# Out-projection of chunks 2 to 5 by a 26-product scheme on 4x4 by 4x2 blocks, with ten right forms made once, stored in DRAM and streamed

## The chip, the cores and the metric

The kernel runs on one core of a Trainium2 chip. The metric is the device time of one execution in microseconds; three executions of the kernel before took 994.28, 994.46 and 996.12 us, and the median, 994.46, is its time. The core has five instruction queues that run at the same time and wait for each other by semaphores: TensorE (PE in the profile; PEld is its weight load), VectorE (DVE), ScalarE (ACT), GpSimd (POOL) and SyncE (SP), which here only issues DMA transfers. SBUF is the on-chip memory that all of them work from; PSUM is the small memory that TensorE writes its products to, in eight banks.

## What is computed

The reference has two parts. A routed attention over 4 batches, 8 heads, 768 positions and 64 columns per head gives a matrix x of 3072 tokens by 512 columns. The second part, which the change touches, is

```python
h = x @ w_in                                   # 3072x512 @ 512x2048
sp = np.maximum(h, 0.0) + np.log1p(np.exp(-np.abs(h)))   # softplus
g = h * erf(sp)
return (g @ w_out).astype(np.float32)          # 3072x2048 @ 2048x512
```

All of it is in fp32. Softplus and erf are two ScalarE tables, and each change of table is an instruction of its own.

## The kernel before

The attention fills the span up to about 410 us. While it runs, the weights are loaded and some of their sums are made. Then comes the second part, in six chunks (`NCHUNK`) of 512 tokens.

**Products by sevens.** Both matrix products are done by a seven-product scheme for matrices cut into 2x2 blocks: seven products of sums of blocks (`ORDER` gives their sequence) take the place of eight products of blocks. `left_forms` and `right_forms` make the sums, four additions each, and put three into new places and one in place of a block. `block` (line 649) runs seven products: for each it takes a PSUM bank, issues the matmuls, evicts the bank as `fresh` or `further` say (copies by ScalarE, additions by VectorE), and then does the next one or two entries of `aside_work`, a list of side work for the other engines that is written out by hand.

**Hidden.** `hidden(n, lot)` (line 668) makes the hidden units of chunk n in one of two lots (halves of the 2048). It has four blocks of seven products, each product two matmul calls. The hidden values lie transposed, features on the partitions, in two tiles `g` per lot, one for each half s of the chunk's tokens. The right operand is x and its three new sums in `x_more`.

**Gate.** `gate` runs softplus and erf on ScalarE over one `g` tile and multiplies on VectorE. `add_hidden` then makes the left sums of the gated values, on VectorE, into a tile `g_more`.

**Project.** `project(n, lot, pace)` (line 720) multiplies by `w_out`: for each s one block of seven products of four matmul calls each, so that a chunk has 2 lots x 2 halves x 7 = 28 products. `w_out` stays in SBUF with block b12 replaced by b22 - b12, and its three new sums stay in `more_out`; these forms are made once, on GpSimd. The second lot is added to the first in `osb`, from where SP stores it.

**Order.** The main loop (line 990) alternates so that a gate always has a stage of matmuls beside it:

```python
project(n, 0, 2 if n else 3)
...
hidden(n + 1, 0)
...
project(n, 1, 2)
...
hidden(n + 1, 1)
```

The sums of the next chunk's x (`right_forms(ve, *x_parts(n + 1))`) are VectorE side work of the first project stage. Each engine runs its instructions in the order in which they are written: the class `InOrder` (line 55) records every operation, which is why nearly all instructions of the profile have line 62, and are told apart by the tiles that they write and read. DMA issues by `nc.sync` are placed by the framework.

Of the kernel before, what the change touches and what calls it, by code (L numbers as in the profile page):

```python
# [2 lines left out]

# [6 lines left out]
F32 = mybir.dt.float32  # L10
# [4 lines left out]
ALU = mybir.AluOpType  # L15
ACT = mybir.ActivationFunctionType
# [3 lines left out]
P = 128  # L20
B, H, S, D = 4, 8, 768, 64
C = 16
# [9 lines left out]
DM, DFF = H * D, 2048  # L32
NFT = DFF // P
CT = 512
NCHUNK = B * S // CT
HT, HK, HF, HM = CT // 2, DM // P // 2, NFT // 2, DM // 2
FG = HF // 2
# [11 lines left out]
LAST_X = 11  # L49
MASKS = {(0, 2): ("k", 0), (2, 0): ("q", 0), (2, 2): ("k", 1), (5, 2): ("q", 1)}  # L50
FIRST_MASKS = {(2, 0): ("k", 0), (2, 1): ("q", 0), (2, 2): ("k", 1), (5, 2): ("q", 1)}


class InOrder:
# [16 lines left out]
def kernel(  # L71
# [10 lines left out]
    nc = tc.nc  # L82

    in_order = [True]
    te, ve, ae, ge = (
        InOrder(tc, e, in_order) for e in (nc.tensor, nc.vector, nc.scalar, nc.gpsimd)
    )

    def pool(name, bufs, **kw):
        return ctx.enter_context(tc.tile_pool(name=name, bufs=bufs, **kw))  # L90
# [3 lines left out]
    dram = pool("dram", 1, space=bass.MemoryType.DRAM)  # L94
# [4 lines left out]
    w_out = const.tile([P, NFT, DM], F32, name="w_out")  # L99
    more_in = const.tile([P, 3, HK, DFF // 2], F32, name="more_in")  # L100
    more_out = const.tile([P, 3, HF, HM], F32, name="more_out")
# [95 lines left out]
    for base, pattern, sign, op, fill in (  # L197
# [5 lines left out]
            out=first, in_=first, compare_op=op, fill=fill, base=base, pattern=pattern,  # L203
# [61 lines left out]
    for e in range(2):  # L265
        for n in range(2):
            r = e * D + n * Q
# [275 lines left out]
    def load_x(n):  # L543
        if n < NCHUNK:
            if n not in x_of:
                x_of[n] = xp.tile([P, DM // P, CT], F32, name="x_own")
            nc.sync.dma_start(
                out=x_of[n], in_=x_dram.rearrange("(k p) t -> p k t", p=P)[:, :, n * CT : (n + 1) * CT]
            )
# [52 lines left out]
    g_of = {}  # L602
# [10 lines left out]
    aside_work = []  # L613
# [49 lines left out]
    def finish_aside():  # L663
        for work in aside_work:
            work()
        aside_work.clear()

    def hidden(n, lot, between={}, pace=1, **kw):

        for s in range(2):  # L670
            g_of[n, s, lot] = gp.tile([P, 2, FG, HT], F32, name="g")
        x = rights(*x_parts(n))
        for j in range(FG):
            w = lefts(*w_in_parts(lot * FG + j, 1))
            a, b = (g_of[n, s, lot] for s in range(2))
            block(
                lambda i: [(w[i][:, k], x[i][:, k]) for k in range(HK)],
                fresh(a[:, 0, j], b[:, 0, j], a[:, 1, j], b[:, 1, j], **kw), pace=pace,
            )
            between.get(j, lambda: None)()  # L680
# [22 lines left out]
    def idle(n):  # L703
        return [lambda: None] * n

    def gates(n, lot, which=(0, 1), between=()):
        work = list(between)
        for s in which:
            curves, products_of = gate(n, lot, s)
            if s == which[0]:  # L710
                work = [curves] + work + idle(7 - len(work)) + products_of
            else:
                work += [curves, *sums, *idle(3)] + products_of
            sums = add_hidden(n, lot, s)
        return work + sums

    out_v = out.rearrange("(n t p) m -> n p t m", p=P, t=2)
    osb_of = {}

    def project(n, lot, pace):  # L720

        w = rights(*w_out_parts(lot * FG, FG))
        for s in range(2):
# [17 lines left out]
            block(lambda i: [(g[i][:, f], w[i][:, f]) for f in range(FG)], after, done, pace)  # L741
            del g_of[n, s, lot], sums_of[n, s, lot]

    def run(work):
        for _ in work:
            pass
# [16 lines left out]
    def period(p, i):  # L763
# [4 lines left out]
        def mask(place):  # L768
            which = (MASKS if p else FIRST_MASKS).get((i, place))
            if which:  # L770
# [108 lines left out]
    for e in range(2):  # L879
        ve.tensor_copy(  # L880
            out=ccT[e * D : (e + 1) * D, :, e * C : (e + 1) * C],
            in_=pct[e * D : (e + 1) * D].rearrange("d (r e c) -> d r e c", e=2, c=C)[:, :, e],
# [7 lines left out]
    for r in (0, D):  # L890
        for half in range(2):
            for e in range(2):
                c = r + half * Q + e * C
                ve.tensor_copy(
                    out=pick[r : r + D, half, e * D : (e + 1) * D].rearrange("p (n c) -> p n c", n=2)[:, :, 1 : C + 1],
                    in_=first[r : r + D, c : c + C].unsqueeze(1).to_broadcast([D, 2, C]),
# [49 lines left out]
    gsp = pool("gsp", 4)  # L946
    actp = pool("actp", 1)
    outp = pool("outp", 2)
# [38 lines left out]
    aside_work += together(idle(2) + gates(0, 0, (0,)), all_weights(4, N_LATE))  # L987
    hidden(0, 1, pace=2, first=ve.tensor_copy)
    finish_aside()
    for n in range(NCHUNK):  # L990
        between = right_forms(ve, *x_parts(n + 1)) if n + 1 < NCHUNK else []
        if n == 0:
            aside_work += gates(0, 0, (1,), between) + gates(0, 1, (0,))
        else:
            aside_work += gates(n, 1, (0, 1), between)
        project(n, 0, 2 if n else 3)
        finish_aside()
        if n == 0:
            aside_work += together(gates(0, 1, (1,)), idle(2) + [fence] + out_forms[2] + out_forms[3])
            hidden(1, 0, first=ve.tensor_copy)  # L1000
        elif n + 1 < NCHUNK:
            hidden(n + 1, 0)
        if n + 1 < NCHUNK:
            finish_aside()
            load_x(n + 2)
            aside_work += gates(n + 1, 0)
        project(n, 1, 2)
        finish_aside()
        if n + 1 < NCHUNK:
            hidden(n + 1, 1)  # L1010
            finish_aside()


# [30 lines left out]
```

## Time and profile before

| What | Before |
|---|---|
| median of three runs | 994.46 us |
| profiled execution, its own time | 994.52 us |
| span of that execution, first to last instruction | 992.8 us |
| TensorE busy, from 409.5 us on | 580.3 of 583.3 us |
| VectorE, ScalarE, GpSimd busy there | 365.0, 200.3, 35.6 us |
| TensorE waits after 412 us | none in the table of waits |
| VectorE: 128x256 eviction from PSUM; 128x512 sum or product in SBUF | 0.42; 0.68 us |
| GpSimd: 128x512 sum of fp32 | 1.27 us |
| ScalarE: table load; 128x2048 softplus or erf; 128x256 copy | 1.28; 1.91; 0.37 us |
| 512 KB load from DRAM; 256 KB store, issue to landing | 3.4 to 4.7; 2.0 us |

TensorE is busy from the first product of the second part to the last, so the other engines' busy shares matter only where TensorE comes to wait for them. A row of the timeline gives start, length, engine, line, operation, the tile written, the tiles read, shapes and a count of equal instructions in a row. In the groups "128x512" counts what one instruction covers. The matmul rows overlap, since matmuls are pipelined; the distance between two starts is what one costs.

### The profile page before, as it was taken

How to read it: one execution, taken by the hardware profiler on the slowest of the kernel's cores; microseconds unless marked ns; L12 is line 12 of the kernel's file. 1: busy time of each engine (PE TensorE's matmuls, PEld its weight loads, DVE VectorE, ACT ScalarE, POOL GpSimd, SP SyncE). 2: the span in 40 equal slices, each digit the busy share in tenths (PEclk: the TensorE clock that was granted, in tenths of full speed). 3: DMA queues.
4: the chain of work that ended last, by engine and by line, in shares of the span. 5: the costliest groups of instructions: out<-in, count | busy, mean ns of one | idle time of the engine just before them, and what ended most of it. 6: DMA issues, size and time to landing. Idle time of an engine off the chain costs nothing.

```text
span 992.8 us, 20557 instructions
## 1 busy us (share of the span) xinstructions
PE 985.6 (99%) x8362; PEld 739.5 (74%) x8362; DVE 709.1 (71%) x1361; ACT 488.1 (49%) x659; POOL 350.6 (35%) x237
## 2 busy tenths in 40 slices
PE   8999999999999999999999999999999999999998
PEld 3555555555555555788888888888888888888887
DVE  8888888888888886889666564756475647655653
ACT  3777777777776665485432414150505050505050
POOL 1688888787888888662400000000000000000000
PEclk9999999999999999999999999999999999999999
DMA  9444444444444210331000100010001000000001
GB/s 217 83 111 108 109 109 111 108 115 108 92 96 110 52 35 18 101 111 61 1 22 22 43 1 22 22 43 1 22 22 43 1 21 22 1 1 22 22 1 42
DMA packets 147294, 55.88 MB, mean 56 GB/s; under 512 B 128640, under 2 KB 137088, under 8 KB 147200
## 3 DMA queue, kind: packets, MB, share of 16 engines
q1 hardware_dynamic: 144848, 54.29, 21.9%
q8 instruction: 65, 1.06, 0.5%
q10 hardware_dynamic: 2352, 0.30, 0.2%
q14 instruction: 29, 0.24, 0.1%
HBM read 41.98 MB, written 12.58 MB: 55 GB/s over the span
## 4 chain that ended last, share of the span: by engine, by line
PE 98%; DVE 1%; DMA 0%; issue 0%; ACT 0%; SPq 0%; DVEq 0%
PE bank L62 44%; PE turned L62 32%; PE sc L62 16%; PE wide L62 6%; DVE nmx L62 1%; DMA in_q<-in_q_dram 0%; DVE sims L62 0%; DVE kT L62 0%; DVE qT L62 0%; DVE km L62 0%; DVE turned L62 0%; DVE nbig L62 0%; ACT qm L62 0%; DVE osb L62 0%; SPq L62 0%
## 5 line engine op out<-in xcount | busy, mean ns | idle before, releaser
L62 POOL TENSOR_TENSOR more_out<-more_out,pr 128x768 f32<-128x768 f32 x128 | 217.2, 1697 | 18.6 <-ACT pr L62 10.1
L62 DVE TENSOR_REDUCE nmx<-wide 128x2 f32<-128x768 f32 x189 | 180.5, 955 | 48.2 <-PE wide L62 47.2
L62 ACT ACTIVATE pr<-sc 128x768 f32<-128x768 f32 x192 | 149.0, 812 | 94.3 <-PE wide L62 78.6
L62 PE MATMUL turned<-pr,in_v 128*32 128x194 f32 x3072 | 145.4, 330 | 0.0
L62 PEld LDWEIGHTS turned<-pr,in_v 128*32 128x32 f32 x3072 | 91.5, 109 | 51.2 <-issue 21.3
L62 DVE TENSOR_TENSOR g<-bank,g 128x256 f32<-128x256 f32 x222 | 89.7, 421 | 53.1 <-PE bank L62 46.3
L62 PE MATMUL bank<-x_own,w_in 128*128 128x256 f32 x424 | 104.4, 379 | 0.0
L62 PE MATMUL bank<-w_out,g 128*128 128x256 f32 x448 | 103.2, 379 | 0.0
L62 PE MATMUL sc<-qT,kT 64*128 64x384 f32 x528 | 98.3, 486 | 0.0
L62 PEld LDWEIGHTS bank<-w_out,g 128*128 128x128 f32 x448 | 85.0, 190 | 11.9 <-DVE g L62 0.4
L62 PEld LDWEIGHTS bank<-x_own,w_in 128*128 128x128 f32 x424 | 80.4, 190 | 11.5 <-issue 0.6
L62 DVE TENSOR_TENSOR osb<-bank,osb 128x256 f32<-128x256 f32 x87 | 35.5, 420 | 72.8 <-ACT osb L62 25.4
L62 ACT COPY g<-bank 128x256 f32<-128x256 f32 x28 | 10.4, 372 | 153.2 <-PE bank L62 148.5
L62 ACT ACT_TABLE_LOAD x48 | 61.6, 1283 | 45.7 <-DVE g L62 45.1
L62 PE MATMUL bank<-x_more,more_in 128*128 128x256 f32 x296 | 76.0, 379 | 0.0
L62 POOL TENSOR_TENSOR more_out<-pr,pr 128x768 f32<-128x768 f32 x32 | 60.3, 1883 | 28.3 <-ACT pr L62 28.3
L62 PEld LDWEIGHTS <-qv 64*128 64x128 bf16 x384 | 27.0, 93 | 52.9 <-issue 36.7
L62 PEld LDWEIGHTS sc<-qT,kT 64*128 64x128 f32 x528 | 50.0, 187 | 21.3 <-ACT inv L62 2.3
L62 PE MATMUL wide<-kv,qv 64*128 64x384 bf16 x378 | 64.1, 328 | 1.3 <-DVE nmx L62 0.6
L62 PE MATMUL bank<-more_out,g_more 128*128 128x256 f32 x272 | 64.3, 379 | 0.0
L62 DVE TENSOR_TENSOR g<-a_s,g 128x512 f32<-128x512 f32 x96 | 62.5, 689 | 1.2 <-ACT a_s L62 1.2
L62 PE MATMUL wide<-km,qm 64*128 64x384 bf16 (+1 forms) x378 | 62.6, 327 | 0.0
(172 smaller groups left out, 1671.7 us busy)
## 6 DMA issues: line engine op xcount, KB each, us to landing
x_own<-in_moe_w_in_dram SPq DMA_DIRECT2D x13, 512.0 KB, 4.5
in_v<-in_v_dram SPq DMA_DIRECT2D x32, 192.0 KB, 3.0
x_dram<-more_out SPq DMA_DIRECT2D x128, 48.0 KB, 2.0
x_own<-x_dram SPq DMA_DIRECT2D x6, 1024.0 KB, 5.2
out_dram<-osb SPq DMA_DIRECT2D x23, 256.0 KB, 2.0
in_k<-in_k_dram SPq DMA_DIRECT2D x59, 96.0 KB, 2.8
in_q<-in_q_dram SPq DMA_DIRECT2D x58, 96.0 KB, 2.8
g_more<-in_moe_w_out_dram SPq DMA_DIRECT2D x6, 512.0 KB, 3.4
```

The lines of the kernel that those rows point to most:

```text
L62: ins = getattr(self.engine, name)(*args, **kw)
```

## The change

Chunks 0 and 1 stay as they were, except that the two project stages of chunk 1 now follow each other. Chunks 2 to 5 run `hidden26(n, 0)`, `hidden26(n, 1)` and then `project26(n)`, one projection for both lots. The gated values of a chunk are taken as 4 token blocks by 4 feature groups (left operands 0 to 15), `w_out` as 4 feature groups by 2 column halves (`w_block` 0 to 7), and the product as 4 by 2 blocks (c 0 to 7). The list `RIGHT` gives for each of 26 products the right operand: a block of `w_out` (negative), one of eight kept forms (0 to 7: six places in `more_out` and two blocks of `w_out` overwritten), or one of ten streamed forms (100 to 109). `LEFT` gives the left operand, which may be one of three extra places (16 to 18). Twenty-eight `LEFT_STEPS` per chunk make left forms in place, each after the product named first in its entry (-3 and -1: before the first product), four on GpSimd (`POOL_STEPS`) and the others on VectorE. `AFTER` says how each product goes into the output: c copies and a adds the bank, C and A do so from another output place or one of three temporaries (8 to 10).

The forms of `w_out` are made once, in the hidden stages of chunk 2 (`forms26`): four GpSimd instructions first put b12 back, then eighteen forms in two pieces each run on GpSimd, or on VectorE for six of them. Ten go by way of a ring of three SBUF places to a DRAM tensor, and in each projection they are loaded back into the ring, three ahead.

In `hidden26` the gate works on half of the four feature blocks of both token halves at a time. The last quarter of the gate is in `project26`: its curves after product 0, its four products of VectorE after products 4 and 5. The x sums of the next chunk move from VectorE to GpSimd, into the projection.

```diff
+KAPPA = {1: (0, 1), 2: (0, 0), 0: (1, 1), 3: (1, 0)}
+FORM_STEPS = [
+    (0, -2, -8, 1, -1), (10, -4, -8, -1, 7), (9, -5, -6, -1, 3), (1, -3, -5, -1, -1), (2, -6, 1, 1, -1),
+    (9, -4, 2, -1, 0), (9, -7, 1, -1, 5), (6, -1, -5, 1, 1), (3, -6, 10, -1, -1), (4, 10, 6, -1, -1),
+    (9, 1, 0, -1, 4), (7, -7, -8, -1, 8), (6, -6, 6, -1, -1), (9, -2, 6, 1, 2), (10, -7, 10, 1, 6),
+    (5, -7, 0, -1, -1), (9, -1, 5, 1, 9), (7, -3, 10, -1, -1),
+]
+VECTOR_FORMS = (3, 4, 6, 10, 15, 16)
+RIGHT = [
+    2, 7, -3, 100, -6, 3, 101, 4, -1, 102, 6, 103, 0,
+    104, -4, -7, 105, 1, 106, 5, 107, -1, 108, -2, -2, 109,
+]
+LEFT = [
+    17, 13, 18, 9, 2, 17, 6, 2, 17, 12, 14, 9, 5,
+    10, 1, 3, 7, 16, 14, 1, 9, 6, 1, 8, 12, 0,
+]
+LEFT_STEPS = [
+    (-3, 16, 2, 10, 1), (-3, 17, 9, 16, 1), (-1, 18, 1, 17, 1), (2, 17, 6, 14, -1), (3, 6, 5, 6, 1),
+    (4, 2, 14, 6, -1), (5, 17, 12, 14, -1), (6, 12, 0, 12, -1), (7, 14, 14, 12, 1), (8, 10, 10, 14, 1),
+    (8, 9, 9, 10, 1), (9, 5, 5, 7, 1), (10, 10, 11, 5, 1), (11, 9, 3, 15, -1), (11, 14, 13, 9, -1),
+    (11, 1, 1, 14, -1), (13, 7, 7, 11, 1), (14, 16, 16, 10, -1), (16, 0, 0, 8, 1), (16, 1, 11, 0, -1),
+    (17, 9, 9, 2, 1), (18, 6, 4, 6, -1), (18, 6, 0, 6, 1), (19, 13, 13, 15, 1), (19, 1, 1, 13, 1),
+    (20, 8, 8, 11, -1), (21, 4, 4, 5, -1), (21, 12, 12, 4, 1),
+]
+POOL_STEPS = (5, 6, 8, 10)
+AFTER = [
...
+    [('c', 9, -1, 1), ('C', 1, 9, 1), ('A', 8, 9, -1), ('A', 5, 8, 1), ('C', 9, 8, -1)],
...
+DONE = {0: 15, 6: 20, 7: 23, 1: 23, 5: 23, 3: 24, 4: 25, 2: 25}
+N_STREAM = 10
+RING = 3
...
+    ring, extra = [], []
+    b_dram = dram.tile([N_STREAM, P, FG * HM], F32, name="b_dram")
+
+    def w_block(b):
+        lot, h = KAPPA[b // 2]
+        f = h * HF + lot * FG
+        return w_out[:, f : f + FG, (b % 2) * HM : (b % 2 + 1) * HM]
+
+    def slot(i):
+        if i < 6:
+            return more_out[:, i // 2, (i % 2) * FG : (i % 2 + 1) * FG]
+        return w_block((4, 7)[i - 6]) if i < 8 else ring[i - 8]
+
+    def flat(t):
+        return t.rearrange("p f m -> p (f m)")
+
+    def take_places():
+        tiles = [
+            gsp.tile([P, 3, FG, P], F32, name="g_more").rearrange("p a j t -> p (a j t)") for _ in range(4)
+        ]
+        for t in tiles[:RING]:
+            ring.append(t[:, 0 : FG * HM].rearrange("p (f m) -> p f m", f=FG))
+            extra.append(t[:, FG * HM :].rearrange("p (j t) -> p j t", j=FG))
+        extra.append([tiles[RING][:, i * HM : (i + 1) * HM] for i in range(3)])
+
+    def forms26():
+        work = []
+        for f in (0, 2, 4, 6):
+            b12, b22 = w_out[:, f : f + 2, HM:], w_out[:, HF + f : HF + f + 2, HM:]
+            work.append(functools.partial(minus_of, b12, b22, b12, ge))
+        turns26 = itertools.cycle((9, 8))
+        for n, (o, a, b, sign, k) in enumerate(FORM_STEPS):
+            o = next(turns26) if o == 9 else o
+            out_, a_, b_ = (slot(x) if x >= 0 else w_block(-1 - x) for x in (o, a, b))
+            form = plus_of if sign > 0 else minus_of
+            engine = ve if n in VECTOR_FORMS else ge
+
+            def piece(f, out_=out_, a_=a_, b_=b_, form=form, engine=engine, k=k):
+                c = slice(f, f + 2)
+                form(out_[:, c], a_[:, c], b_[:, c], engine)
+                if f and k >= 0:
+                    nc.sync.dma_start(out=b_dram[k].rearrange("p (f m) -> p f m", f=FG), in_=out_)
+
+            work += [functools.partial(piece, f) for f in (0, 2)]
+        return work
+
+    def load_stream(k):
+        nc.sync.dma_start(out=flat(ring[k % RING]), in_=b_dram[k % N_STREAM])
+
+    def left26(n, i):
+        if i >= 16:
+            return extra[i - 16]
+        lot, h = KAPPA[i % 4]
+        t = i // 4
+        return g_of[n, t // 2, lot][:, h, :, (t % 2) * P : (t % 2 + 1) * P]
+
+    def left_step(n, x):
+        _, o, a, b, sign = LEFT_STEPS[x]
+        form = plus_of if sign > 0 else minus_of
+        form(left26(n, o), left26(n, a), left26(n, b), ge if x in POOL_STEPS else ve)
+
+    def gate26(n, lot, half):
+        gs = [g_of[n, s, lot][:, :, 2 * half : 2 * half + 2].rearrange("p h j t -> p h (j t)") for s in range(2)]
+        box = []
+
+        def curves():
+            t = actp.tile([P, 2 * FG * HT], F32, name="a_s")
+            box.append(t)
+            for s in range(2):
+                ae.activation(
+                    out=t[:, s * 1024 : (s + 1) * 1024].rearrange("p (h j) -> p h j", h=2),
+                    in_=gs[s], func=ACT.Softplus,
+                )
+            ae.activation(out=t, in_=t, func=ACT.Erf)
+
+        def product(s, h):
+            c = slice((2 * s + h) * 512, (2 * s + h + 1) * 512)
+            ve.tensor_tensor(out=gs[s][:, h], in0=box[0][:, c], in1=gs[s][:, h], op=ALU.mult)
+
+        return curves, [functools.partial(product, s, h) for s in range(2) for h in range(2)]
+
+    def gate_work(n, lot, half):
+        curves, products_of = gate26(n, lot, half)
+        return [curves, *idle(8), *products_of]
+
+    def hidden26(n, lot, generation=()):
+        generation = list(generation)
+
+        def paired(work):
+            if not generation:
+                return work
+            both = []
+            for w in work + idle(14 - len(work)):
+                g = generation[:1]
+                del generation[:1]
+                both.append(lambda w=w, g=g: [f() for f in (w, *g)])
+            return both
+
+        def middle():
+            finish_aside()
+            aside_work.extend(paired(gate_work(n, lot, 0)))
+
+        if lot:
+            aside_work.extend(paired(gate_work(n, 0, 1)))
+        else:
+            aside_work.extend(paired([]))
+        hidden(n, lot, {1: middle})
+        finish_aside()
+        return generation
+
+    def project26(n):
+        for s in range(2):
+            osb_of[n, s] = outp.tile([P, 2, DM], F32, name="osb")
+        temps = extra[3]
+
+        def c_at(i):
+            if i >= 8:
+                return temps[i - 8]
+            t = i // 2
+            return osb_of[n, t // 2][:, t % 2, (i % 2) * HM : (i % 2 + 1) * HM]
+
+        curves, gate_products = gate26(n, 1, 1)
+        gate_products = [gate_products[i] for i in (3, 1, 0, 2)]
+        between = right_forms(ge, *x_parts(n + 1)) if n + 1 < NCHUNK else []
+        for p, r in enumerate(RIGHT):
+            m = bank()
+            lhs = left26(n, LEFT[p])
+            g26 = N_STREAM * (n - 2) + r - 100
+            rhs = ring[g26 % RING] if r >= 100 else slot(r) if r >= 0 else w_block(-1 - r)
+            for f in range(FG):
+                te.matmul(m, lhsT=lhs[:, f], rhs=rhs[:, f], start=(f == 0), stop=(f == FG - 1))
+            if r >= 100:
+                if g26 + RING < N_STREAM * (NCHUNK - 2):
+                    load_stream(g26 + RING)
+            for x, step in enumerate(LEFT_STEPS):
+                if step[0] == p:
+                    left_step(n, x)
+            for op, d, src, sign in AFTER[p]:
+                dst = c_at(d)
+                source = m if op in "ca" else c_at(src)
+                if op in "cC":
+                    if 1 <= p < 6:
+                        if sign > 0:
+                            ve.tensor_copy(out=dst, in_=source)
+                        else:
+                            ve.tensor_scalar(out=dst, in0=source, scalar1=-1.0, scalar2=None, op0=ALU.mult)
+                    elif sign > 0:
+                        ae.copy(out=dst, in_=source)
+                    else:
+                        ae.activation(out=dst, in_=source, func=ACT.Copy, scale=-1.0)
+                else:
+                    (plus_of if sign > 0 else minus_of)(dst, dst, source)
+            if p == 0:
+                curves()
+            if p in (4, 5):
+                for f in gate_products[(p - 4) * 2 : (p - 4) * 2 + 2]:
+                    f()
+            if p in (12, 13, 14, 15) and between:
+                between.pop(0)()
...
+            if p == 12:
+                load_x(n + 2)
...
-    for n in range(NCHUNK):
+    for n in range(2):
         between = right_forms(ve, *x_parts(n + 1)) if n + 1 < NCHUNK else []
         if n == 0:
             aside_work += gates(0, 0, (1,), between) + gates(0, 1, (0,))
@@ -998,17 +1233,30 @@
         if n == 0:
             aside_work += together(gates(0, 1, (1,)), idle(2) + [fence] + out_forms[2] + out_forms[3])
             hidden(1, 0, first=ve.tensor_copy)
-        elif n + 1 < NCHUNK:
-            hidden(n + 1, 0)
-        if n + 1 < NCHUNK:
             finish_aside()
-            load_x(n + 2)
-            aside_work += gates(n + 1, 0)
+            load_x(2)
+            aside_work += gates(1, 0)
         project(n, 1, 2)
         finish_aside()
-        if n + 1 < NCHUNK:
-            hidden(n + 1, 1)
+        if n == 0:
+            hidden(1, 1)
             finish_aside()
+            load_x(3)
+    take_places()
+    generation = forms26()
+    for n in range(2, NCHUNK):
+        generation = hidden26(n, 0, generation)
+        generation = hidden26(n, 1, generation)
+        for work in generation:
+            work()
+        generation = []
+        if n == 2:
+            for k in range(RING):
+                load_stream(k)
+        for x, step in enumerate(LEFT_STEPS):
+            if step[0] < 0:
+                left_step(n, x)
+        project26(n)
 
 
 # ---- launch: one core; inputs and outputs as the reference has them ----
```

## The prediction

> **What bounds the kernel now.** I read the busy times first, then the chain that ended last, then the engines' timelines in the last three fifths of the span, where the change lies.
>
> ```profile
> PE 985.6 (99%) x8362; PEld 739.5 (74%) x8362; DVE 709.1 (71%) x1361; ACT 488.1 (49%) x659; POOL 350.6 (35%) x237
> ...
> PE 98%; DVE 1%; DMA 0%; issue 0%; ACT 0%; SPq 0%; DVEq 0%
> ```
>
> TensorE sets the end: it is 98% of the chain, and the table of waits has no wait of TensorE at all after 412 us. So a product taken away is worth its whole length, and any new wait of TensorE is added in full. TensorE's timeline gives the length:
>
> ```profile
> 747.88 1.89 PE L62 MATMUL bank<-w_out,g 128*128 128x256 f32 x8
> 749.61 1.89 PE L62 MATMUL turned<-w_out,g 128*128 128x256 f32 x8
> ```
>
> A product of the out-projection is 8 matmul records and starts 1.73 us after the one before. VectorE's timeline at the end of a hidden stage shows how late the last eviction is (the next TensorE stage began at 699.54):
>
> ```profile
> 699.74 0.42 DVE L62 TENSOR_TENSOR g<-g,bank 128x256 f32<-128x256 f32 x1 [0.44 <-PE bank L62]
> ```
>
> (That is 0.20 us after TensorE has gone on; here nobody waits for it.) The third reading is VectorE beside GpSimd, two timelines of the same stretch:
>
> ```profile
> 396.45 2.12 DVE L62 TENSOR_TENSOR more_in<-w_in 128x512 f32<-128x512 f32 x1
> 398.60 2.06 DVE L62 TENSOR_TENSOR more_in<-more_in,w_in 128x512 f32<-128x512 f32 x1
> ...
> 449.75 1.72 DVE L62 TENSOR_TENSOR g_more<-g 128x512 f32<-128x512 f32 x1
> ...
> 451.73 0.67 DVE L62 TENSOR_TENSOR g_more<-g_more,g 128x512 f32<-128x512 f32 x1
> ```
>
> ```profile
> 396.34 3.78 POOL L62 TENSOR_TENSOR more_out<-more_out,pr 128x768 f32<-128x768 f32 x2 [0.32 <-ACT pr L62]
> ...
> 449.63 1.30 POOL L62 TENSOR_TENSOR w_out<-w_out,osb 128x512 int32<-128x512 int32 x1 [4.49 <-DVE w_out L62]
> ```
>
> The same 128x512 operation on VectorE takes 0.67 us alone and 1.72 to 2.12 beside GpSimd. At 449.75 it ends 0.55 after GpSimd's (449.63 + 1.30 = 450.93, against 451.47). GpSimd pays too: its two 768-wide instructions take 3.78 where two alone take 3.39 (mean 1697 ns in the groups). In the old kernel this costs nothing, because after 494 us GpSimd does no work.
>
> **What the Trainium skill says.** "SBUF — State Buffer", section "Who interferes with whom": a VectorE instruction with two SBUF inputs contends with a GpSimd instruction that reads SBUF; one with at most one SBUF input doesn't. The rows above agree (2.12 against 0.67), and evictions from PSUM stay at 0.42 beside GpSimd. "TensorE: Matmul & The Clock Gate", section "What's actually happening": after an idle window of some 3.4 us the array runs at half its clock until a busy window has passed. No trace of before shows it, as TensorE never rests there.
>
> **The change, part by part.** I laid the built program's order out engine by engine and gave each instruction the duration of its nearest row; the places below are from that table.
>
> *Removed.* A chunk's out-projection has 26 products for 28: 2 x 1.727 = 3.45 us, in four chunks **-13.8 us**. Hidden products are the same 56 per chunk.
>
> *The first product's left operand (four times).* Before, a hidden stage and the next project stage overlap, since another lot was always ready. Now the first product reads form 17, the second of two sums that stand on VectorE behind the last eviction, and behind the last gate product of the lot. Counting from where TensorE would have gone on: the eviction starts at 0.20 in the row above, but a 512-wide gate product, placed between evictions, pushes it to about 0.83; form 16 starts 0.34 later (1.17), form 17, which needs it, 0.72 later (1.89) and ends at 2.57; a weight load of 0.19 and the handover make 2.8. Nothing covers it, for TensorE's queue is in order: 4 x 2.8 = **+11.2 us**. Bounds: 2.0 each if the gate product is out of the way, 3.3 if one more eviction is in it.
>
> *GpSimd inside the projection (chunks 2 to 4).* Four left steps and, new there, the four right forms of the next chunk's x run on GpSimd at 1.27 us each. The x forms wait for no product, so they follow the last left step at once, though they are written at products 12 to 15. VectorE has in this stretch, products 9 to 13, about five instructions with two SBUF inputs that each meet one of GpSimd's. A pair then takes 1.27 - 0.13 + 0.55 = 1.7 instead of 0.34 to 0.60, so 5 x 1.1 = 5.6 us late. What is late next: three dependent left steps (form 9, 14, 1), of which the third is the left operand of product 14, wanted there with some 0.9 us to spare. Evictions have eight banks (8 x 1.73 = 13.8 us) of cover; a left step has none. About 0.5 us of it is already lost in two small waits at products 11 and 12. So 3.6 at product 14 and 0.5 before it: 3 x 3.6 + 4 x 0.5 = **+12.8 us**. The old trace has no such stretch, so the bounds are wide: 0 if the five miss each other, some 19 if GpSimd's pairs run at 2.1 as they did with 768 columns. Chunk 5 has no x forms, and only the 0.5.
>
> *The ten stored forms, once, in chunk 2.* 28 GpSimd instructions and 12 of VectorE go along hidden(2,0) and hidden(2,1), 48.4 us of TensorE. GpSimd alone needs 28 x 1.27 = 36 us. But after eight of them it stands still for some 8 us until VectorE makes the form that its ninth needs, which in VectorE's order lies behind 15 or so evictions (13 us after the stage began). The other 20, half of them at 1.23 from start to start and half at 1.7 beside VectorE's two-input work, take about 28, so they end 41 us into the stage. VectorE's next-to-last form writes a ring slot whose earlier content must have been stored. That store stands on SP behind a load that waits for another store: GpSimd's form, 15 or 16 of the 20, ends at 34.6, store 3.2, load issue, store 3.2 gives 41.4 (the trace shows 3.4 for 512 KB loads and 2.0 for 256 KB stores; a 512 KB store I put at 3.2, between 2.6 and 4). VectorE reaches that form at about 37 and is held 4.6 us; behind it in its queue stand the evictions of this hidden stage. Eight banks of 0.86 us cover 6.9, and VectorE had lost some of that to GpSimd already, so TensorE loses about 4.5 us inside the stage. Then the gate of the lot's first half starts late, its ScalarE chain (two table loads of 1.28, two softplus of 1.03 by the 0.86 ns per element of the rows, erf of 1.91: 6.5 us) holds the copy that the last seven products' evictions start from, and VectorE has seven evictions, four gate products and two sums after it, some 6 us. TensorE waits about 7.7 at the chunk's first product, of which 2.8 is counted: 4.5 + 4.9 = **+9.4 us**. Bounds: 3 if the stores take 2.6 and the port costs half, 14 if they take 4.
>
> *That wait and the clock.* 7.7 us of idle hold a whole window, so by the skill the next 3.4 us or more run at half clock. Bounds: 0 and 3.4; I take **+2 us** (an estimate from that page).
>
> *Edits at nothing.* Streamed right forms: each load is issued at least 6 products ahead (10 us against 3.4). Stores of the output: VectorE work finished, SP free. The last gate in products 0 to 5: table loads, softplus and erf end at about 9 us, VectorE reaches the gate products at product 4 (8.6), GpSimd's step for product 8 ends near 13.5 of 13.8. If that cover goes, product 8 waits some tenths, which are in the 0.5 above. VectorE's load in a projection, 40 instructions at 0.34 to 0.46 and 26 at 0.60 to 0.72, is 33 of 45 us. Leaving out hidden(2,0) between the two projections of chunk 1 costs nothing: its gates are done three products before they are read. At the end two dependent sums instead of one before the last store: **+0.8 us**.
>
> *Sum.* -13.8 + 11.2 + 12.8 + 9.4 + 2 + 0.8 = **+22.4 us**. The profiled execution took 994.52 us, 1.7 more than its span of 992.8, and stands 0.06 from the median, 994.46. 994.5 + 22.4 = 1016.9; I forecast **1016 us**.
>
> **The rivals.**
>
> *A, the port doesn't bite.* If GpSimd's instructions fall where VectorE works from PSUM, the 12.8 goes to nothing and the hold inside chunk 2's hidden stage to about 0.5; the late gate still costs 4.9. Then -13.8 + 11.2 + 5.4 + 0.8 = +3.6, with the clock perhaps +2: 998 to 1001. For it: many VectorE instructions read PSUM. Against it: 26 of a projection's VectorE instructions are 512 wide with two SBUF inputs, and the doubled rows above.
>
> *B, the left steps are in time (faster).* One mechanism: VectorE runs so far ahead at each projection that its left steps come before TensorE asks for them, so only the bare chain at the opening is left, 2 us a chunk: -13.8 + 8 + 0.8, that is 989.5 us. It decides once all waits of TensorE in the four chunks together stay under 13.8 us. Against it: the opening alone, which no early work can shorten because VectorE's order is fixed, takes 8 to 11 of the 13.8.
>
> *C, the clock falls at more gaps.* If waits of 2.8 to 3.6 also let the clock drop, up to seven more losses of 1.7: 1022 to 1029. Against it: these waits hardly fill one window of 3.4.
>
> *D, the change saves no products.* The order of the built program has 104 matmul instructions per projection for 112, so this one is out.
>
> **How the numbers follow.** The port's cost as worked out, 0.64: 1007 to 1022 (stalls of chunk 2 and of product 14 from half to one and a quarter of the value, clock 0 to 3.4). A 0.19: 997 to 1004. B 0.08: 987 to 994. C 0.09. The range that leaves out 2 in 10 runs from 999 to 1024, as A's lower part and B lie below it and C's upper part above. A difference under 0.2%, 2 us, can't be told from none with this kernel. Faster by more than that is most of B: 0.07; within it, the rest of B and the lowest edge of A: 0.05; slower 0.88.
>
> **What would show each step.** TensorE's matmul records fall by 64 (2 products x 8 x 4). The table of waits, empty for TensorE now, shows waits on VectorE's `g_more` near 2.8 us in chunks 3 to 5 and near 7 in chunk 2, and on `g` of 3 to 4 us in three projections but not in the last. VectorE's 128x512 rows with SBUF inputs have means over 0.9 where GpSimd works. If TensorE's waits sum to less than 20 us, the port was priced too high; if the opening waits are under 2 us, VectorE's order is not what I read; if TensorE waits for DMA in the projections, the stream was too slow, which I don't expect.

## The result, and where the 30 us came from

The changed kernel takes 1024.51 us, the median of four runs (1023.75 to 1026.41), against 994.44 for the kernel before: a ratio of 1.0301, 95% interval 1.0283 to 1.0319. That is 30.1 us slower, where 22 were forecast, and 0.5 us above the range, which is less than the runs differ among themselves. The profiled span went from 992.8 to 1022.9 us, also 30.1.

The page of the changed kernel, busy times first and then the chain that ended last by engine:

```profile
PE 984.6 (96%) x8298; PEld 731.3 (71%) x8298; DVE 769.6 (75%) x1421; ACT 511.8 (50%) x735; POOL 430.4 (42%) x293
...
PE 84%; DVE 9%; issue 2%; POOL 2%; ACT 1%; DMA 1%; SPq 0%; DVEq 0%; POOLq 0%; ACTq 0%
```

TensorE has 64 matmul records fewer (8298 for 8362), yet its busy time fell by 1.0 us only, not by the 13.8 that 64 matmuls at 0.216 us take. That points to matmuls that run slower, though the ends of matmuls are modelled, so that busy time alone can't say by how much. And the chain, 98% TensorE before, now passes for 9% of the span through VectorE. The table of waits of TensorE after 412 us, empty before, reads (us in total, times, longest; `bank` and `turned` are PSUM tiles that a product is written to):

```profile
PE bank L120 <- DVE g_more L120: 11.1, 3, 6.2
PE turned L120 <- DVE g L120: 8.8, 2, 5.4
PE bank L120 <- DVE g L120: 6.7, 2, 3.4
PE turned L120 <- DVE g_more L120: 2.5, 1, 2.5
PE bank L120 <- ACT g L120: 0.5, 1, 0.5
```

The `g_more` rows are the openings of the four projections. The `g` rows are product 14 of chunks 2 to 4, three waits of 3.4, and one of 5.4 inside chunk 2's hidden stage. TensorE's timeline at product 14 of chunk 2 and at the opening of chunk 3:

```profile
695.98 3.30 PE L120 MATMUL turned<-w_out,g 128*128 128x256 f32 x8 [3.37 <-DVE g L120]
699.08 2.28 PE L120 MATMUL bank<-w_out,g 128*128 128x256 f32 x8
...
769.42 1.99 PE L120 MATMUL bank<-more_out,g_more 128*128 128x256 f32 x8 [2.45 <-DVE g_more L120]
771.25 1.03 PE L120 MATMUL bank<-w_out,g 128*128 128x256 f32 x4
```

A product of 8 records, 1.73 us from start to start before, takes 3.10 (695.98 to 699.08) behind the first wait and 1.83 behind the second. The 3.10 is a second cost, on top of the wait.

**The opening.** VectorE's timeline just before 769.42: the last eviction, form 16, then forms 17 and 18 in one line. The first product reads form 17, so TensorE has nothing to do until the first of these two has ended.

```profile
767.63 0.41 DVE L120 TENSOR_TENSOR g<-g,bank 128x256 f32<-128x256 f32 x1
767.96 0.68 DVE L120 TENSOR_TENSOR g_more<-g 128x512 f32<-128x512 f32 x1
768.68 1.42 DVE L120 TENSOR_TENSOR g_more<-g,g_more 128x512 f32<-128x512 f32 x2
```

**The port.** VectorE ahead of product 14, and GpSimd in the same stretch with its four sums of the next chunk's x:

```profile
687.08 1.75 DVE L120 TENSOR_TENSOR g<-g 128x512 f32<-128x512 f32 x1
688.76 0.41 DVE L120 TENSOR_TENSOR g_more<-g_more,bank 128x256 f32<-128x256 f32 x1
689.09 1.42 DVE L120 TENSOR_TENSOR g<-g 128x512 f32<-128x512 f32 x1
690.43 2.89 DVE L120 TENSOR_TENSOR g_more<-g_more 128x256 f32<-128x256 f32 x2
```

```profile
686.84 1.45 POOL L120 TENSOR_TENSOR x_more<-x_own 128x512 f32<-128x512 f32 x1
688.36 1.60 POOL L120 TENSOR_TENSOR x_more<-x_own,x_more 128x512 f32<-128x512 f32 x1
689.92 1.71 POOL L120 TENSOR_TENSOR x_own<-x_own 128x512 f32<-128x512 f32 x1
691.60 1.44 POOL L120 TENSOR_TENSOR x_more<-x_more,x_own 128x512 f32<-128x512 f32 x1
```

A left step that takes VectorE 0.68 alone takes 1.75 and 1.42 here, and a pair of 128x256 sums 2.89 where a pair takes about 0.75 elsewhere. The eviction at 688.76 reads one operand from PSUM and keeps its 0.41. This is the contention of the prediction: (1.75 - 0.68) + (1.42 - 0.68) + (2.89 - 0.75) = 3.95 us of lateness in four instructions.

**The stored forms.** SP's queue in chunk 2's hidden stages:

```profile
637.17 3.68 SPq L844 DMA_DIRECT2D b_dram<-g_more  x2
641.04 0.32 SPq L850 DMA_DIRECT2D g_more<-b_dram  x1
641.47 0.69 SPq L844 DMA_DIRECT2D b_dram<-g_more  x1
```

VectorE's form that fills a ring slot, and the form that takes the same slot again once its content is stored:

```profile
630.13 1.75 DVE L120 TENSOR_TENSOR g_more<-more_out 128x512 f32<-128x512 f32 x1
...
647.12 0.69 DVE L120 TENSOR_TENSOR g_more<-w_out,more_out 128x512 f32<-128x512 f32 x1 [5.93 <-DMA b_dram<-g_more]
```

The store of the form of 630.13 is the one issued at 641.47. It was late twice. The form had ended at 631.88, but two stores of GpSimd's forms went ahead of it on SP's queue, the second of them issued at 640.53 when GpSimd had finished that form, and then a load: 9.6 us in all. And it took 5.56 us from issue to landing, as the third 512 KB transfer within 1 us; the three other stores from ring slots between 625 and 667 us took 2.60 to 2.91. VectorE, which came to its form at 641.2, stood 5.93 us with the evictions of the hidden stage behind it.

**The clock.** The mean granted clock fell from 1.000 to 0.988. TensorE in windows of 3.41 us, laid so that each begins where the record of the clock may change (the changes listed below lie 5, 15, 45 and 96 times 3.413 us after 645.24; columns: window, length, busy and matmuls, granted clock, DMA share, GB/s):

```profile
693.03:696.44 3.41, 0.46 (x2) 1.00 0.51 154
696.44:699.85 3.41, 3.41 (x9) 0.50 0.00 0
...
897.83:901.24 3.41, 1.58 (x7) 1.00 0.33 129
901.24:904.65 3.41, 3.41 (x17) 1.00 0.00 0
969.51:972.92 3.41, 1.41 (x7) 1.00 0.01 2
972.92:976.33 3.41, 3.41 (x10) 0.50 0.00 0
```

The first two lines and the middle two are product 14 of chunks 2 and 4, with the same wait of 3.53 us: behind the one, the next window runs at half clock, with 9 matmuls in place of 17; behind the other it doesn't. The shorter wait of 2.70 at chunk 5's opening halves it again. In all the record shows half clock in 645.24 to 652.07, 662.31 to 669.14 and in three single windows from 696.44, 798.84 and 972.92. TensorE had work in 3.9, 3.1 and 3 x 3.4 us of these, and half of that, 8.6 us, is lost.

The account, from the starts of matmuls (a gap is the time from one start to the next, less 0.22):

| Step of the prediction | forecast, us | measured, us |
|---|---|---|
| 2 products fewer in each of four chunks | -13.8 | -13.8 |
| first left operand | +11.2 | +10.5 (2.61, 2.61 and 2.70 in chunks 3 to 5, and 2.6 of chunk 2's 6.39) |
| GpSimd in the projection | +12.8 | +11.9 (three of 3.53, and 0.33 in each chunk before it) |
| stored forms in chunk 2 | +9.4 | +10.3 (0.23, 0.71 and 5.58 inside the hidden stages, and 3.8 of the opening) |
| clock | +2 | +8.6 |
| tail behind the last matmul | +0.8 | +1.15 (3.40 to 4.55) |
| not forecast | | +1.4 (by difference: the last matmul starts 28.9 us later, 1018.33 for 989.40; 16 starts that come about 0.1 us late, most of them just behind a wait, make up 1.5) |
| sum | +22.4 | +30.1 |

### The profile page after: what moved, and what is told of

It reads as the page before. It is cut to its first block, busy times and chain, and to the rows that moved or that the text cites. A ratio compares the mean times of both kernels' runs of the same rounds, so it can differ in the third digit from the quotient of the medians.

```text
span 1022.9 us, 20786 instructions
## 1 busy us (share of the span) xinstructions
PE 984.6 (96%) x8298; PEld 731.3 (71%) x8298; DVE 769.6 (75%) x1421; ACT 511.8 (50%) x735; POOL 430.4 (42%) x293
## 3 DMA queue, kind: packets, MB, share of 16 engines
q8 instruction: 65, 1.06, 0.4%
## 4 chain that ended last, share of the span: by engine, by line
PE 84%; DVE 9%; issue 2%; POOL 2%; ACT 1%; DMA 1%; SPq 0%; DVEq 0%; POOLq 0%; ACTq 0%
PE bank L120 35%; PE turned L120 28%; PE sc L120 16%; PE wide L120 5%; DVE g L120 4%; DVE g_more L120 2%; DVE osb L120 1%; DVE nmx L120 1%; ACT a_s L120 1%; POOL w_out L120 1%; POOL g_more L120 1%; DMA b_dram<-g_more 1%; ACT L120 1%; POOL more_out L120 0%; DMA in_q<-in_q_dram 0%
## 5 line engine op out<-in xcount | busy, mean ns | idle before, releaser
L120 POOL TENSOR_TENSOR g<-g 128x512 f32<-128x512 f32 x12 | 15.7, 1306 | 301.5 <-ACT a_s L120 204.5
L120 PE MATMUL bank<-w_out,g 128*128 128x256 f32 x352 | 84.8, 391 | 6.7 <-DVE g L120 6.7
L120 PEld LDWEIGHTS bank<-x_own,w_in 128*128 128x128 f32 x424 | 80.2, 190 | 12.8 <-ACT g L120 0.9
L120 PEld LDWEIGHTS bank<-w_out,g 128*128 128x128 f32 x352 | 69.3, 198 | 17.9 <-issue 7.5
L120 DVE TENSOR_TENSOR g<-a_s,g 128x512 f32<-128x512 f32 x96 | 69.9, 745 | 1.2 <-ACT a_s L120 1.2
L120 DVE TENSOR_TENSOR g<-g 128x512 f32<-128x512 f32 x84 | 62.9, 749 | 1.1
L120 POOL TENSOR_TENSOR w_out<-w_out 128x512 f32<-128x512 f32 x14 | 20.9, 1508 | 99.1 <-PE turned L120 77.9
```

The source lines that it names most:

```text
L120: ins = getattr(self.engine, name)(*args, **kw)
```

## The experiments

All are edits of the changed kernel. The kernel before ran beside each group with medians of 994.24 to 994.34 us.

### Keep TensorE busy in its waits

```diff
+            for _ in range((13 if n == 2 else 5) if p == 0 else (7) if p == 14 and n + 1 < NCHUNK else 0):
+                te.matmul(m, lhsT=w_in[:, 0, 0:P], rhs=w_in[:, 0, 0:HT], start=True, stop=True)
             for f in range(FG):
                 te.matmul(m, lhsT=lhs[:, f], rhs=rhs[:, f], start=(f == 0), stop=(f == FG - 1))
```

> In the projection of chunks 2 to 5, calls without use (128 columns by 256, operands long in SBUF, into the bank that the next product overwrites) are put ahead of the waiting product: 13 at chunk 2's opening, 5 at the other three, 7 ahead of product 14 in chunks 2, 3 and 4. TensorE is busy while it would wait; the waits of the products themselves end no sooner. Theory (the halved clock is a cost of its own): the half-clock stretches at 662, 696, 798 and 972 us go, the one at 645 us in chunk 2's hidden stage stays, so 1.6 + 1.7 + 1.7 + 1.6 = 6.6 us less: 1018 us, clock near 0.996. Rival (the lower clock falls in time in which TensorE would have waited anyway, and the whole loss is the waits): 1024 us within 1; up to 3 us more if the calls hold up a product that was ready.

Measured: 1017.84 us, four runs from 1017.76 to 1018.25, ratio to before 1.0237 (1.0221 to 1.0252); clock 0.996. TensorE does 98 matmuls more and the kernel is 6.7 us faster. Its timeline at product 14 of chunk 2:

```profile
691.29 3.19 PE L120 MATMUL turned<-w_in 128*128 128x256 f32 x14
694.75 1.99 PE L120 MATMUL turned<-w_out,g 128*128 128x256 f32 x8 [0.27 <-DVE g L120]
696.58 1.89 PE L120 MATMUL bank<-w_out,g 128*128 128x256 f32 x8
```

The left form came as late as before: the seven calls, 14 records, fill the wait, and 0.27 us of it remain. But the product behind it takes 1.83, not 3.10, and up to the last matmul the record shows half clock only at 646.68, in chunk 2's hidden stage, where no bank is free for such calls. So the halved clock is a cost of its own, 6.7 us in four of the five stretches, and the rival falls.

### Fill the waits in part

The same edit, with one call at the openings of chunks 3 and 4, two at chunk 5's, and two, three and four ahead of product 14.

> As the run with calls put into the waits, but each wait is filled in part, to leave TensorE idle for different times: at the openings of chunks 3 and 4 one call (2.2 us left), of chunk 5 two (1.75 left), of chunk 2 all 13; ahead of product 14 two calls in chunk 2 (2.7 left), three in chunk 3 (2.2 left), four in chunk 4 (1.8 left). Theory (the clock is halved when about 2.0 us or more of one 3.4 us window are idle, so that it hangs on where a wait falls in the windows): none of the waits of 1.8 us or less lowers the clock; of those of 2.2 to 2.7 us some do and some don't. Time 1019 to 1023 us. Rival (it takes a stretch without any matmul, of a fixed length above 2.7 us): no half clock outside chunk 2's hidden stage, 1018 us.

Measured: one run, 1017.97 us, 1 us below the range expected by the theory; clock 0.996. Gaps of 2.18, 2.18 and 1.84 us at the openings of chunks 3 to 5, of 2.58, 2.15 and 1.72 at product 14, and no half clock outside chunk 2's hidden stage up to the last matmul. Two of the windows with the most idle time:

```profile
690.24:693.65 3.41, 1.64 (x8) 1.00 0.46 151
...
864.32:867.73 3.41, 1.53 (x7) 1.00 0.03 5
```

No wait was long enough in one window; the expected drops among those over 2.0 us didn't come. By itself the run agrees with the rival as well, whose 1018 it met. The rival is put out by other runs: waits of 2.61 and 2.70 us did halve the clock in three kernels, and equal waits in the same kernels did not. And six waits of 1.7 to 2.6 us cost no more here than their own time: 26 calls do what 49 did.

### Make the three first left forms earlier

```diff
         def middle():
             finish_aside()
-            aside_work.extend(paired(gate_work(n, lot, 0)))
+            work = gate_work(n, lot, 0)
+            if lot:
+                work[1:4] = [functools.partial(left_step, n, x) for x in range(3)]
+            aside_work.extend(paired(work))
...
-        for x, step in enumerate(LEFT_STEPS):
-            if step[0] < 0:
-                left_step(n, x)
         project26(n)
```

> The three left forms made ahead of the projection (16, 17 and 18) are issued in the middle of the second hidden stage, behind its first curves, and not behind its last evictions. Theory (they are late because VectorE comes to them last): the waits of 2.61, 2.61 and 2.71 us at the openings of chunks 3 to 5 go, chunk 2's 6.39 falls to about 1.5 (there VectorE is held by the stored forms), and the half-clock stretches at 662 and 972 us go with them (3.2): 7.9 + 4.9 + 3.2 = 16 us less, 1008 to 1009 us. Rival (VectorE has no room earlier, so that the three sums, 0.75 us each, make the banks of the hidden stage late instead): at least half of it comes back as waits inside the second hidden stages, 1016 to 1022 us.

Measured: 1008.64 us (1008.57 to 1010.12), ratio 1.0148 (1.0131 to 1.0165): 15.9 us less. The table of waits of TensorE has no `g_more` left:

```profile
PE turned L120 <- DVE g L120: 8.7, 2, 5.3
PE bank L120 <- DVE g L120: 6.7, 2, 3.4
PE bank L120 <- ACT g L120: 0.5, 1, 0.5
```

All four opening waits are gone, chunk 2's 6.39 whole, and nothing came back in the hidden stages: VectorE's sums at 749.31, 750.25 and 751.18 take 0.68 each between its evictions. The first theory holds. The clock gained less than the two stretches: chunk 4's wait at product 14, as long as before, now falls into another place of its window and halves the clock, which it did not do in the changed kernel. So the 16 us were met by two misses that cancel: 14.3 us of waits went where 12.8 were expected, and about 1.6 us of clock where 3.2 were.

```profile
884.20:887.61 3.41, 1.12 (x5) 1.00 0.38 143
887.61:891.02 3.41, 3.41 (x9) 0.50 0.00 0
```

### The sums of x on VectorE, and later on GpSimd

```diff
-        between = right_forms(ge, *x_parts(n + 1)) if n + 1 < NCHUNK else []
+        between = right_forms(ve, *x_parts(n + 1)) if n + 1 < NCHUNK else []
```

> The four sums of the next chunk's x are made by VectorE at the same places (behind products 12 to 15), so that GpSimd has only the four left steps in the projection. Theory (VectorE's left steps on two SBUF operands are held by GpSimd's x sums on the port that both use): the wait of 3.53 us ahead of product 14 goes in chunks 2 to 4 although VectorE gets 4 x 0.7 us more to do, and the half-clock stretches at 696 and 798 us go too: 10.6 + 3.4 = 14 us less, 1010 to 1011 us. Rival (VectorE simply has too much between products 11 and 14; GpSimd is not to blame): VectorE's extra 2.8 us make the wait longer, up to 5 or 6 us in each of three chunks: 1029 to 1032 us.

Measured: 1010.34 us (1010.15 to 1011.57), ratio 1.0163 (1.0148 to 1.0178): 14.2 us less, although VectorE has 12 instructions more to do. VectorE in the stretch that was slow:

```profile
687.63 0.68 DVE L120 TENSOR_TENSOR g<-g 128x512 f32<-128x512 f32 x1
...
689.16 0.74 DVE L120 TENSOR_TENSOR g_more<-g_more 128x256 f32<-128x256 f32 x2
```

What took 1.75 and 2.89 us is back at 0.68 and 0.74, and product 14 has no wait in any chunk. The rival, a VectorE with too much to do, asked for 5 us more in three chunks. The other way to part the two engines gives the same:

```diff
-            if p in (12, 13, 14, 15) and between:
-                between.pop(0)()
+            if p == 21 and between:
+                t = up.tile([P, HM], F32, name="u")
+                g = left26(n, 12)[:, 0, 0:1]
+                ge.tensor_tensor(out=t[:, 0:1], in0=g, in1=g, op=ALU.add)
+                for form in between:
+                    form()
```

> The four sums of the next chunk's x stay on GpSimd, but come at product 21, behind a GpSimd operation on one column that reads the last left form made before it, so that they run when VectorE has no left step left. Theory (port): the wait ahead of product 14 goes in three chunks and with it the half-clock stretches at 696 and 798 us: 14 us less, 1010 to 1011 us, unless x is late for the next hidden stage, which would show as a wait at its opening. Rival (the four left steps on GpSimd are what holds VectorE, not the x sums): the wait stays within 1 us of 3.5, 1022 to 1025 us.

Measured: 1010.75 us (1010.21 to 1011.33), ratio 1.0165 (1.0149 to 1.018): 13.8 us less, no wait at product 14, none at the next hidden stage. The left steps that stay on GpSimd are not what held VectorE there.

### Stores ahead of loads

```diff
-                    nc.sync.dma_start(out=b_dram[k].rearrange("p (f m) -> p f m", f=FG), in_=out_)
+                    sy.dma_start(out=b_dram[k].rearrange("p (f m) -> p f m", f=FG), in_=out_)
...
-        nc.sync.dma_start(out=flat(ring[k % RING]), in_=b_dram[k % N_STREAM])
+        sy.dma_start(out=flat(ring[k % RING]), in_=b_dram[k % N_STREAM])
```

> Stores of the ten forms and the loads that stream them are kept in program order on SP's queue, so that all ten stores are issued ahead of the first three loads. Theory (VectorE waits 5.93 us at 647.12 us of the trace for a store that went out at 641.47, behind a load of 512 KB, and took 5.56 us; the other stores of that stretch took 2.8): the store goes out with no load ahead of it, VectorE's wait falls to about 3, TensorE's gap of 5.58 us to about 2.8, and one of the two half-clock windows there goes: 3 to 5 us less, 1020 to 1021.5 us. Rival (the forms on GpSimd and VectorE are late themselves, the store only comes last): within 1 us of 1024.5.

Measured: 1018.42 us (1018.08 to 1018.9), ratio 1.0241 (1.0226 to 1.0257): 6.1 us less, more than expected. SP's queue and VectorE's form:

```profile
631.91 0.33 SPq L120 DMA_DIRECT2D b_dram<-g_more  x1
...
637.18 7.73 SPq L120 DMA_DIRECT2D b_dram<-g_more  x3
647.65 1.27 SPq L120 DMA_DIRECT2D g_more<-b_dram  x3
```

```profile
641.12 1.16 DVE L120 TENSOR_TENSOR g_more<-w_out,more_out 128x512 f32<-128x512 f32 x1
```

VectorE's wait is not 3 us but nothing, and TensorE's gap of 5.58 falls to 1.31. The theory saw only the load ahead of the store. In program order the store of VectorE's form also goes ahead of the two stores of GpSimd's forms: it is issued at 631.91, 9.6 us earlier, and has landed at 634.64, long before VectorE wants its slot at 641.12. Part of it is given back: the opening of chunk 2 grows from 6.39 to 7.62, since VectorE waits 3.98 us for ScalarE's gate there as it did before. All gaps together fall by 3.0 us (31.2 to 28.2 for those over 0.4); the rest is clock, of which seven half-clock windows became four: the pair at 645.24 is gone, and chunk 3's product 14 and chunk 5's opening no longer halve it, chunk 4's product 14 now does.

### Leave the making of the right forms out

```diff
-            work.append(functools.partial(minus_of, b12, b22, b12, ge))
+            work.append(lambda: None)
...
-                form(out_[:, c], a_[:, c], b_[:, c], engine)
                 if f and k >= 0:
-                    nc.sync.dma_start(out=b_dram[k].rearrange("p (f m) -> p f m", f=FG), in_=out_)
+                    nc.sync.dma_start(out=b_dram[k].rearrange("p (f m) -> p f m", f=FG), in_=w_block(k % 8))
```

> The operations that make the right forms in chunk 2's hidden stages are left out (all on GpSimd and VectorE; the ten stores go out with blocks of the weights as they are), so the products are taken with other numbers; nothing else moves. Theory (the waits inside chunk 2's hidden stages and the part of its opening over 2.6 us come from these operations and the stores that they wait for): no wait of TensorE over 0.3 us before chunk 2's projection, its opening 2.6 us, no half clock at 645 us and not two windows at 662: 6.5 + 3.8 + 3.6 = 14 us less, 1010 to 1011 us. Rival (the waits come from the hidden stage's new order, with the gate split in halves, and the forms are hidden): the waits near 641 and 648 us stay, 1020 us or more.

Measured: one run, 1009.04 us, 15.5 less. TensorE has no gap over 0.4 us in chunk 2's hidden stages, chunk 2's opening is 2.61 like the others, and the half clock at 645 and 662 is gone. So the gaps inside and the excess of the opening come from making the forms and from the stores that wait for them. The 1.5 us beyond expectation fit the clock: three half-clock windows were expected to stay, at two of product 14 and at chunk 5's opening, and two did, at product 14 of chunks 2 and 4.

### All three edits in one, and a step further

The edits of the early left forms, the late sums of x and the stores ahead of loads in one kernel:

> The three edits in one kernel: left forms 16 to 18 made in the middle of the second hidden stage, the sums of the next chunk's x on GpSimd at product 21, stores and stream loads in program order. Theory (each takes away a cost of its own, the clock's included): 15.9 + 13.8 + 3 to 5 us less than 1024.5, so 990 to 992 us, 2 to 4 us under the kernel before; about 5 us of waits of TensorE left, in chunk 2, and no half clock in the projections. Rival (the gains overlap, since every edit moves work of the same two engines): 996 us or more, no gain on the kernel before.

Measured: 987.54 us (five runs, 987.45 to 987.58), ratio to before 0.9931 (0.9919 to 0.9944), below the expected range, as the stores gave 6.1 us where 3 to 5 were counted. One by one the edits gave 15.9 + 13.8 + 6.1 = 35.8 us, together 37.0, so the savings add up to within 1.2 us, and the clock is at 1.000. What TensorE still waits for by the table of waits is all in chunk 2: 1.4 us for GpSimd's left step ahead of product 8, and 1.1 and 0.6 for VectorE and ScalarE in the hidden stage.

The next edit takes GpSimd out of the left steps:

```diff
-POOL_STEPS = (5, 6, 8, 10)
+POOL_STEPS = ()
-VECTOR_FORMS = (3, 4, 6, 10, 15, 16)
+VECTOR_FORMS = (3, 4, 6, 10, 14, 15, 16)
```

> The kernel of three edits, with the four left steps that GpSimd had given to VectorE, and one of the right forms (the 15th of 18) moved from GpSimd to VectorE. Theory (GpSimd's 1.3 us a step is now the last wait: 0.2 us in each chunk, 1.5 us at product 8 in chunk 2, 1.3 us in its hidden stage): 1 to 2 us less than 987.5, 985.5 to 986.5 us. Rival (VectorE has no room for 4 x 0.7 us more between its evictions): 988 us or more.

Measured: 985.90 us (five runs, 985.59 to 985.96), ratio to before 0.9915 (0.9901 to 0.9929); beside the same kernel before, 8.4 us faster than it. VectorE takes four more left steps in each chunk, and TensorE's waits are still all in chunk 2:

```profile
PE bank L120 <- DVE g L120: 1.1, 2, 0.6
PE bank L120 <- DVE g_more L120: 0.8, 1, 0.8
PE turned L120 <- DVE g L120: 0.4, 1, 0.4
```

So most of the saving of the 26 products can be had. By the account's terms: -13.8, then 3.0 for the gaps left in chunk 2 (over 0.4 us each) and 1.2 for the tail (4.57 against 3.40) make -9.6, and the span fell by 8.6 (992.8 to 984.2); the last 1.0 us is, by the starts of the matmuls, gaps under 0.4 us each: two of about 0.3 and seven of about 0.1.

## Why the prediction was wrong in size

**Right.** The direction, the three places of the waits and their sizes: 2.8 forecast at the openings and 2.6 to 2.7 found, 3.6 at product 14 and 3.53 found in three chunks and not in the last, about 7.7 at chunk 2's opening and 6.39 found. Each cause was then shown by taking it away: the left forms' place behind the last evictions, GpSimd's sums of x on the port, the making of the forms. "If the opening waits are under 2 us" and "TensorE waits for DMA in the projections" did not come. Rivals A and B fall with that: the port bites, and TensorE's waits came to 29.6 us where B needed less than 13.8. The opening "which no early work can shorten", held against B, holds only for the order as built: with the three forms earlier in VectorE's order it went altogether.

**Right in part by luck.** The 3.6 at product 14 does not follow from its own line: 5.6 us late, less 0.9 to spare and 0.5 lost before, leaves 4.2. The lateness itself was well judged: by VectorE's timeline six instructions lost 5.9 us, the 3.95 above and 0.91 and 1.06 in two 128x256 sums before them. Two more figures are loose: ten sums at 1.23 and ten at 1.7 are 29.3 us and not "about 28", and the sum of 1016.9 was put down as 1016.

**Right in mechanism, partly off.** "The ten stored forms": the held store was foreseen, also that it stands behind a load and another store, but priced at 3.2 us twice with a hold of 4.6. The store waited for GpSimd's form ahead of it on the queue, then took 5.56, and held VectorE for 5.93; the 4.5 us inside the stage became 6.5, and the opening's extra was 3.8 for 4.9. The sum, 10.3 for 9.4, hides that.

**Wrong.** The step "That wait and the clock". It gave the clock to one wait only, chunk 2's 7.7 us, at +2 with bounds of 0 and 3.4, because "these waits hardly fill one window of 3.4". It read the Trainium skill's page "TensorE: Matmul & The Clock Gate", section "What's actually happening", as if an idle window had to be empty. That section also says that the window is free-running; what it does not say is how much of it must be idle. The runs show about three fifths: a wait of 2.7 us was enough at 969.51 to 972.92, where 1.41 us of 3.41 were busy. Five stretches cost 8.6 us, where +2 was put; filling four of them with work brought 6.7 back. That difference, 6.6 us, is most of the 7.7 between forecast and result in the account. Rival C said it, 1022 to 1029, and got 0.09; its argument against itself was the same one sentence. The range ended too low for the same reason: the port's part of it, up to 1022, took the clock at 3.4 at most, and C's upper part was left out.

**Not seen.** The 1.4 us that the account leaves over: the starts of matmuls that come 0.1 us late, at 769.42 behind the opening of chunk 3 for one. Why a start behind a wait is late by that much stays open.

## What to carry to other kernels

When a change turns an unbroken run of matmuls into one with waits of some 2.6 us or more, price each wait twice: its length, and the chance of one 3.4 us window at half clock behind it, 1.7 us. Ahead of a wait that can't be removed, a few matmuls of no use into a bank that is overwritten anyway are worth their issue; here they took 6.7 us off. A faster scheme on TensorE moves its sums to the other engines: ask where each operand's last sum stands in its engine's queue, which other engine shares the port at that moment, and what stands ahead of a store on its queue.

## What the runs showed of the hardware

- **The half clock needs no empty window.** Take windows of 3.413 us from one change of the clock record on, and the idle time in each from the starts of the matmuls (gaps of over 0.1 us), in the ten kernels from 610 us to the last matmul. Of the windows at full clock, none with 58% idle or less was followed by half clock; of three with 59 or 60%, one was; all 22 with 62% or more were. Of the windows at half clock, where a matmul counts as 0.43 us of work, all ten that were idle for 59% or more were followed by another, and none of the 23 with 18% or less was. So waits of 2.6 to 3.5 us cost or don't cost 1.7 us more by where they fall, and an edit elsewhere in the kernel moves them. What exactly is counted in a window isn't settled by these runs.
- **Both sides pay on the port.** GpSimd's 128x512 sum, 1.27 us alone, took 1.44 to 1.71 while VectorE's took 1.42 to 1.75 for 0.68. The Trainium skill's page "SBUF — State Buffer", section "Who interferes with whom", names the contention; the sizes are from these rows.
- **Transfers of 512 KB issued within 1 us of each other on one queue landed one after another, whichever way they went.** In the changed kernel a store, a load and a store issued at 640.53, 641.04 and 641.47 took 2.91, 4.64 and 5.56 us from issue to landing. With the stores in program order three loads issued at 647.65, 648.09 and 648.54 took 3.22, 4.37 and 5.48. So the 5.56 looks like the price of the third place, rather than of a store behind a load.
